# Gate branch as one dense first stage in SBUF, queries made ahead, then attention alone

## The chip, the cores and the metric

The kernel runs on one core of one Trainium2 chip, as one program. The metric is the device time of one execution in microseconds (us), from the first to the last instruction of the core. Lower is better.

## The reference

The input is 2048 tokens of width 512. One layernorm feeds two branches, and the output is `x + s * g`.

```python
x  = A_x                                   # (1, 2048, 512), bf16
xn = layernorm(x)
# branch A, attention: 32 heads of 128, 2048 cached keys and values per head
q  = (xn @ wq) split into heads
p  = softmax(q @ k_cache^T * 128**-0.5)
s  = concat_heads(p @ v_cache) @ wo        # (2048, 512)
# branch B, the gate: token mixer and MLP
h  = gelu(layernorm(xn) @ w1)              # 512 -> 512, tanh form of GELU
hs = [h0 shifted by +1 token, h1 by -1, h2 by +2, h3 by -2] @ w2   # four channel groups of 128
x1 = xn + hs
x2 = x1 + gelu(layernorm(x1) @ w3) @ w4    # 512 -> 1792 -> 512
g  = silu(x2)
out = x + s * g
```

## The kernel before

**Attention.** The work is cut into 128 units, `units`: eight groups `g` of four heads, in each group four blocks `qt` of 512 query tokens, in each block the four heads `hh`. A unit has eight slots, and one loop over `n` walks all slots in order; the program keeps that order on every engine. A slot p of unit u (`s_slot`) makes two score matmuls of 512 columns (`ps_s`, weights from `kT`) and one Exp on ScalarE over the pair, 128x1024, from PSUM into `pT` (L187). Two PSUM buffers hold `ps_s`, so the scores of a slot wait for the Exp two slots earlier. Five slots later (`LAG`) `pv_slot` multiplies by `vb` into `ps_o`.

**Softmax sums.** DVE adds the four `pT` tiles of a unit into `acc` (`add_first`, `add_next`, `add_last`: L193, L198 twice, L203, L204). At p = 3 of the next unit `sums` makes four one-column matmuls with `acc` as weights (`ps_sum`), takes the reciprocal, and sends it through DRAM (`dr`) so that it comes back broadcast to all partitions (`rb`). `norm` (L237) multiplies `ps_o` by `rb` into `oT` at p = 2 of the unit after.

**Queries and output.** `q_mm` makes the query of unit u+1 with four matmuls at p = 0 and 1, and DVE copies it at p = 2 (`q_copy`, L173). When the four heads of a block are done, `wo_mm` and `wo_post` multiply one token tile per unit by `wo` at p = 4 to 6 and add it to `s_acc` (L265); in the last group `wo_post` also multiplies by the gate and adds x (L269, L271) and stores the output. `ps_q`, `ps_sum` and `ps_wo` share one PSUM buffer, tag `xa`.

**The gate.** All matmuls of the mixer and the MLP are cut into 136 chunks (`m1_chunk`, `m2_chunk`, `m3_chunk`, `m4_chunk`) of four or five matmuls, which the slot loop places at p = 2 and 3 or 6 and 7 of units 5 to 119, in PSUM buffer `xm`. A GELU chunk is copied from PSUM by ScalarE (`pre`, L369), and `gelu_pair` then computes the tanh form for a pair of chunks over the next slots: Square on ScalarE (L339), a polynomial on DVE (L343), Tanh on ScalarE (L348), a product on DVE (L351). The layernormed tokens, x1 and the gate each pass through DRAM (`xn_d`, `x1_d`, `g_d`) by DMAs that GpSimd issues; w3 is loaded again for each block of 512 tokens, w4 once.

**Start.** Four token tiles are normalized and transposed by matmuls (`first_tokens`, copies to `xnT` on ScalarE, L314), and the first query is made. Keys are loaded by transposing DMAs on SP's queue (L142). The other twelve token tiles are normalized between the slots of units 0 to 11 and transposed by DMA (L302).

Of the kernel before, what the change touches and what calls it, by code (L numbers as in the profile page):

```python
# [17 lines left out]
def kernel(  # L18
# [15 lines left out]
    nc = tc.nc  # L34
# [7 lines left out]
    assert Dh == P and D % P == 0 and Sq % 512 == 0 and Sk % (2 * P) == 0  # L42
    assert F % (2 * P) == 0 and D == 4 * P
# [7 lines left out]
    HG = 4 if H % 4 == 0 else (2 if H % 2 == 0 else 1)  # L51
# [20 lines left out]
    s_acc = const.tile([P, NT, D], FP32, name="s_acc")  # L72
    ones_t = const.tile([P, 1], BF16, name="ones_t")
    nhalf = const.tile([P, 1], FP32, name="nhalf")
    mv2 = const.tile([P, NT, nc.vector.BN_AGGR_DIM], FP32, name="mv2")
    rstd2 = const.tile([P, NT], FP32, name="rstd2")
    nc.vector.memset(ones_t[:], 1.0)
    nc.vector.memset(nhalf[:], -0.5)
    ident = const.tile([P, P], BF16, name="ident")
    diag = const.tile([P, P], FP32, name="diag")  # L80
    pin(nc.gpsimd.iota(diag[:], pattern=[[-1, P]], base=0, channel_multiplier=1,
# [15 lines left out]
    tokp = ent(pool("tok", 4))
    mp = ent(pool("mp"))
    drp = ent(pool("drp", 4, bass.MemoryType.DRAM))
    dsp = ent(pool("dsp", 1, bass.MemoryType.DRAM))  # L100
    psS = ent(pool("psS", 2, PSUM))
    psO = ent(pool("psO", 2, PSUM))
    psX = ent(pool("psX", 1, PSUM))

    xsrc = x2d.rearrange("(t p) d -> t p d", p=P)
    wq_v = A_wq.rearrange("(dc p) j -> p dc j", p=P)
    w3_v = B_w3.rearrange("(dc p) f -> p dc f", p=P)
    xn_d = [dsp.tile([P, D], BF16, name=f"xn_d{t}") for t in range(NT)]
    x1_d = [dsp.tile([P, D], BF16, name=f"x1_d{t}") for t in range(NT)]
    g_d = [dsp.tile([P, D], BF16, name=f"g_d{t}") for t in range(NT)]  # L110

    def mm(out, lhsT, rhs, start, stop):
        pin(nc.tensor.matmul(out=out, lhsT=lhsT, rhs=rhs, start=start, stop=stop))  # L113

    def rsqrt(out, var):
        ve = smp.tile([P, 1], FP32, name="ve")
        pin(nc.gpsimd.tensor_scalar(out=ve[:], in0=var, scalar1=EPS, scalar2=None, op0=ALU.add))
        pin(nc.gpsimd.tensor_tensor(out=out, in0=ve[:], in1=nhalf[:], op=ALU.pow))
# [40 lines left out]
    def load_wo(h):  # L159
        wos[h] = wop.tile([P, D], BF16, name="wo_h")  # L160
        pin(nc.sync.dma_start(out=wos[h][:], in_=A_wo[h * Dh:(h + 1) * Dh, :]))

    def q_mm(u, dcs):
        g, qt, hh = units[u]
        if dcs[0] == 0:
            st[u] = dict(psq=psX.tile([P, 512], FP32, tag="xa", name="ps_q"))
        for dc in dcs:
            mm(st[u]["psq"][:], wqs[g * HG + hh][:, dc, :],
               xnT[:, dc, qt * 512:(qt + 1) * 512], dc == 0, dc == DC - 1)

    def q_copy(u):
        qT = qtp.tile([P, 512], BF16, name="qT")
        pin(nc.vector.tensor_copy(out=qT[:], in_=st[u].pop("psq")[:]))  # L173
        st[u]["qT"] = qT

    def s_slot(u, p):
# [7 lines left out]
        if p % 2 == 0:  # L184
            s.setdefault("pT", []).append(ptp.tile([P, 4, 512], BF16, name="pT"))
# [20 lines left out]
    def pv_slot(u, p):  # L206
        g, qt, hh = units[u]
        s = st[u]
        if p == 0:
            s["o"] = psO.tile([P, 512], FP32, name="ps_o")  # L210
# [16 lines left out]
    def bcast(u):  # L227
        st[u]["rb"] = rp.tile([P, 512], FP32, name="rb")
# [11 lines left out]
    wo_box = {}  # L240

    def wo_mm(g, t, hhs):
        if hhs[0] == 0:
            wo_box[0] = psX.tile([P, D], FP32, tag="xa", name="ps_wo")
# [7 lines left out]
    def fin_load(t):  # L252
        xl = tokp.tile([P, D], BF16, tag="ta", bufs=8, name="xl")
        nc.gpsimd.dma_start(out=xl[:], in_=xsrc[t])
        gl = tokp.tile([P, D], BF16, tag="ta", bufs=8, name="gl")
        nc.gpsimd.dma_start(out=gl[:], in_=g_d[t][:])
        fin[t] = (xl, gl)

    def wo_post(g, t):
        ps = wo_box.pop(0)  # L260
        sa = s_acc[:, t, :]
        if g == 0:
            pin(nc.vector.tensor_copy(out=sa, in_=ps[:]))
            return
        pin(nc.vector.tensor_tensor(out=sa, in0=ps[:], in1=sa, op=ALU.add))  # L265
        if g < NG - 1:
            return
        xl, gl = fin.pop(t)
        pin(nc.vector.scalar_tensor_tensor(  # L269
            out=gl[:], in0=sa, scalar=0.5, in1=gl[:], op0=ALU.mult, op1=ALU.mult))  # L270
        pin(nc.vector.tensor_tensor(out=xl[:], in0=gl[:], in1=xl[:], op=ALU.add))  # L271
# [3 lines left out]
    ln = {}  # L275

    def ln1_load(t, eng):
        xin = tokp.tile([P, D], BF16, tag="ta", bufs=8, name="xin")
        pin(eng.dma_start(out=xin[:], in_=xsrc[t]))
        ln[t] = xin  # L280

    def ln1_stats(t):
        xin = ln[t]
        bn = smp.tile([P, nc.vector.BN_STATS_DIM], FP32, name="bn")
        mv = smp.tile([P, nc.vector.BN_AGGR_DIM], FP32, name="mv")
        rs = smp.tile([P, 1], FP32, name="rs")
# [5 lines left out]
    def ln1_norm(t):
        xin, mv, rs = ln.pop(t)
        xn = tokp.tile([P, D], BF16, tag="tb", bufs=8, name="xn")
        pin(nc.vector.tensor_scalar(
            out=xn[:], in0=xin[:], scalar1=mv[:, 0:1], scalar2=rs[:],
            op0=ALU.subtract, op1=ALU.mult))
        return xn

    def ln1_apply(t):  # L300
        xn = ln1_norm(t)
        pin(nc.sync.dma_start_transpose(out=xnT[:, :, t * P:(t + 1) * P], in_=xn[:]))  # L302
        pin(nc.gpsimd.dma_start(out=xn_d[t][:], in_=xn[:]))

    def first_tokens():
        xns = [ln1_norm(t) for t in range(4)]
        st[0] = dict(psq=psX.tile([P, 512], FP32, tag="xa", name="ps_q"))
        psq = st[0]["psq"]
        for t in range(4):
            tp = psO.tile([P, DC, P], FP32, tag="ps_o", name="ps_o")  # L310
            for dc in range(DC):
                mm(tp[:, dc, :], xns[t][:, dc * P:(dc + 1) * P], ident[:], True, True)
            ts = slice(t * P, (t + 1) * P)
            pin(nc.scalar.activation(out=xnT[:, :, ts], in_=tp[:], func=ACT.Identity))  # L314
            if t >= 1:
                q_part(t - 1, psq)
        q_part(3, psq)
        qT = qtp.tile([P, 512], BF16, name="qT")
        pin(nc.vector.tensor_copy(out=qT[:, 0:3 * P], in_=psq[:, 0:3 * P]))
        pin(nc.vector.tensor_copy(out=qT[:, 3 * P:], in_=psq[:, 3 * P:]))  # L320
        st[0].pop("psq")
        st[0]["qT"] = qT
        for t in range(4):
            pin(nc.gpsimd.dma_start(out=xn_d[t][:], in_=xns[t][:]))

    def q_part(t, psq):
        ts = slice(t * P, (t + 1) * P)
        for dc in range(DC):
            mm(psq[:, ts], wqs[0][:, dc, :], xnT[:, dc, ts], dc == 0, dc == DC - 1)


    mlp = {}

    def gelu_pair(pre, dest, n):
        sq = gtp.tile([P, 2, 512], BF16, name="sq")
        f2 = "p a f -> p (a f)"

        def square():
            pin(nc.scalar.activation(  # L339
                out=sq[:], in_=pre[:], func=ACT.Square, scale=GELU_A ** 0.5))  # L340

        def poly():
            pin(nc.vector.scalar_tensor_tensor(  # L343
                out=sq[:].rearrange(f2), in0=sq[:].rearrange(f2), scalar=1.0,
                in1=pre[:].rearrange(f2), op0=ALU.add, op1=ALU.mult))

        def tanh():
# [338 lines left out]
```

## Time and profile before

| what | value |
|---|---|
| three runs | 1300.81, 1303.24, 1305.64 us; median 1303.24 |
| profiled execution, first to last instruction (span) | 1303.1 us |
| granted TensorE clock, mean over the span | 0.994 |
| TensorE / ScalarE / DVE / GpSimd busy | 1267.1 / 1113.9 / 1024.7 / 146.4 us |
| matmuls | 6236 |
| DMA | 111.76 MB, mean 86 GB/s |

The span is the profiled execution's own time; it lies within the three runs. In the profile's rows PE is TensorE's matmul pipeline, PEld its weight loads, DVE is VectorE, ACT is ScalarE, POOL is GpSimd and SP is SyncE; a q behind an engine's name means its instruction queue, for instance where it issues a DMA. A row of a timeline has the start and the length of a group of like instructions, both in us, and in brackets the idle time before it and what ended it. A row of the groups has the count, the busy time in us, the mean of one in ns and the idle time before. A row of the table of stretches has the stretch, its length, then busy time and count for PE, PEld, DVE, ACT and POOL, then the granted clock, the DMA share and GB/s. All matmuls have one line, since one helper makes them; they are told apart by their tiles.

### The profile page before, as it was taken

Reading aid. Unit: us, or ns where it says so; the run is one execution under the profiler, and the core shown is the slowest. Engines: PE = TensorE matmul, PEld = TensorE weight load, DVE = VectorE, ACT = ScalarE, POOL = GpSimd, SP = SyncE. Lnnn points to the kernel's source line nnn. Section 1 sums busy time; section 2 is a strip of 40 time slices with the busy share of each in tenths; the row PEclk is TensorE's granted clock in tenths of the full one; section 3 lists DMA queues with packets and bytes.
Section 4 is the critical chain, followed back from the end, with each engine's and each line's share of the span. In section 5 each row is a group of like instructions: output and inputs, shape, how many; then the busy total and the mean of one; then the engine's idle time right before and its main releaser. Section 6 shows DMA issues by size and latency. Waiting matters only on the chain.

```text
span 1303.1 us, 17205 instructions
## 1 busy us (share of the span) xinstructions
PE 1267.1 (97%) x6236; PEld 608.7 (47%) x6236; DVE 1024.7 (79%) x1404; ACT 1113.9 (85%) x1189; POOL 146.4 (11%) x259
## 2 busy tenths in 40 slices
PE   7898999999999999999999999999999999999995
PEld 3444444444444444444444444444444444444442
DVE  5787788888788777788887778888777878777886
ACT  6888998887899988899988889998889999888882
POOL 4223002333111100000001000000000000000110
PEclk9999999999999999999999999999999999999997
DMA  7735343356432555224553245424444224422322
GB/s 174 150 85 118 67 85 89 80 132 138 102 73 81 98 106 90 48 66 81 93 98 62 55 94 87 90 49 86 73 84 91 41 58 76 91 61 54 81 71 71
DMA packets 174292, 111.76 MB, mean 86 GB/s; under 512 B 127040, under 2 KB 151104, under 8 KB 174208
## 3 DMA queue, kind: packets, MB, share of 16 engines
q1 hardware_dynamic: 162176, 82.36, 32.7%
q0 software_dynamic: 9632, 27.54, 8.3%
q10 hardware_dynamic: 2400, 0.79, 0.3%
q8 instruction: 48, 0.79, 0.3%
q14 instruction: 36, 0.29, 0.1%
HBM read 81.53 MB, written 8.65 MB: 69 GB/s over the span
## 4 chain that ended last, share of the span: by engine, by line
PE 83%; DVE 6%; ACT 5%; DMA 3%; issue 1%; SPq 0%; POOL 0%; ACTq 0%; DVEq 0%; POOLq 0%
PE ps_s L113 30%; PE ps_o L113 28%; PE ps_m L113 9%; PE ps_wo L113 9%; PE ps_q L113 7%; ACT pT L187 3%; DVE acc L198 2%; DMA rb<-dr 1%; PE ps_sum L113 1%; ACT sq L339 1%; DMA dr<-rc 1%; DMA kT<-in_A_k_cache_dram 1%; DVE s_acc L265 1%; DVE acc L203 1%; ACT pre L369 1%
## 5 line engine op out<-in xcount | busy, mean ns | idle before, releaser
L187 ACT ACTIVATE pT<-ps_s 128x1024 bf16<-128x1024 f32 x1024 | 1014.7, 1029 | 156.4 <-PE ps_s L113 154.0
L113 PE MATMUL ps_s<-qT,kT 128*128 128x512 bf16 x2048 | 610.0, 380 | 3.8 <-DMA kT<-in_A_k_cache_dram 2.2
L113 PE MATMUL ps_o<-pT,vb 128*128 128x512 bf16 x2048 | 608.3, 379 | 1.3 <-DVE oT L237 1.3
L198 DVE TENSOR_TENSOR acc<-acc,pT 128x2048 bf16<-128x2048 bf16 x256 | 312.2, 1220 | 55.5 <-ACT pT L187 49.7
L113 PEld LDWEIGHTS <-kT 128*128 128x128 bf16 x2048 | 227.0, 113 | 226.0 <-issue 17.6
L113 PEld LDWEIGHTS <-vb 128*128 128x128 bf16 x2048 | 200.0, 98 | 227.0 <-issue 1.6
L193 DVE TENSOR_TENSOR acc<-pT 128x2048 bf16<-128x2048 bf16 x128 | 155.9, 1218 | 29.5 <-ACT pT L187 29.5
L113 PE MATMUL ps_wo<-wo_h,oT 128*128 128x512 bf16 x512 | 154.3, 385 | 8.1 <-DVE oT L237 3.9
L113 PE MATMUL ps_q<-xnT,wq_h 128*128 128x512 bf16 (+1 forms) x524 | 154.1, 379 | 4.9 <-DVE acc L204 2.7
L265 DVE TENSOR_TENSOR s_acc<-ps_wo,s_acc 128x512 f32<-128x512 f32 x112 | 77.2, 690 | 93.5 <-PE ps_wo L113 93.4
L237 DVE TENSOR_TENSOR oT<-ps_o,rb 128x512 bf16<-128x512 f32 x128 | 87.1, 681 | 7.6 <-DMA rb<-dr 7.6
L173 DVE CAST qT<-ps_q 128x512 bf16<-128x512 f32 x127 | 87.0, 685 | 7.1 <-PE ps_q L113 7.1
L203 DVE TENSOR_TENSOR acc<-acc 128x1024 bf16<-128x1024 bf16 x128 | 88.6, 692 | 4.4
L113 PEld LDWEIGHTS <-oT 128*128 128x128 bf16 x512 | 50.4, 99 | 73.0 <-issue 11.9
L113 PEld LDWEIGHTS <-wq_h 128*128 128x128 bf16 x524 | 51.7, 100 | 66.8 <-issue 6.6
L113 PE MATMUL ps_m<-xn2T,w_sb 128*128 128x512 bf16 x224 | 66.5, 378 | 0.0
L113 PE MATMUL ps_m<-w_sb,h2T 128*128 128x512 bf16 x224 | 64.0, 379 | 0.0
L488 POOL DMA_DIRECT2D w_sb<-in_B_w_dram x28 | 21.1, 755 | 352.7 <-PE ps_m L113 327.2
L204 DVE TENSOR_TENSOR acc<-acc 128x512 bf16<-128x512 bf16 x128 | 54.4, 425 | 4.4
L113 PEld LDWEIGHTS <-acc 128*128 128x128 bf16 x512 | 37.0, 115 | 36.4 <-DVE acc L204 6.2
L223 DVE RECIPROCAL rc<-ps_sum 128x4 f32<-128x4 f32 x128 | 22.9, 179 | 37.7 <-PE ps_sum L113 36.7
L520 POOL DMA_DIRECT2D g_d<-xr x16 | 8.7, 546 | 350.5 <-DVE xr L518 350.5
(54 smaller groups left out, 569.6 us busy)
## 6 DMA issues: line engine op xcount, KB each, us to landing
rb<-dr SPq DMA_DIRECT2D x128, 256.0 KB, 4.4
vb<-in_A_v_cache_dram SPq DMA_DIRECT2D x64, 256.0 KB, 4.7
w_sb<-in_B_w_dram POOLq DMA_DIRECT2D x28, 256.0 KB, 4.1
wo_h<-in_A_wo_dram SPq DMA_DIRECT2D x32, 128.0 KB, 4.1
wq_h<-in_A_wq_dram SPq DMA_DIRECT2D x28, 128.0 KB, 4.6
kT<-in_A_k_cache_dram SPq DMA_TRANSPOSE x128, 4.7
xn_d<-xn POOLq DMA_DIRECT2D x16, 128.0 KB, 4.3
dr<-rc SPq DMA_DIRECT2D x128, 2.0 KB, 1.4
```

The source lines that it names most:

```text
L113: pin(nc.tensor.matmul(out=out, lhsT=lhsT, rhs=rhs, start=start, stop=stop))
L173: pin(nc.vector.tensor_copy(out=qT[:], in_=st[u].pop("psq")[:]))
L187: pin(nc.scalar.activation(out=s["pT"][-1][:, jj:jj + 2, :], in_=sps[:], func=ACT.Exp, scale=SCALE))
L193: pin(nc.vector.tensor_tensor(out=s["acc"][:], in0=s["pT"][0][:], in1=s["pT"][1][:], op=ALU.add))
L198: pin(nc.vector.tensor_tensor(out=a[:], in0=a[:], in1=st[u]["pT"][i][:], op=ALU.add))
L203: pin(nc.vector.tensor_tensor(out=a[:, 0:2, :], in0=a[:, 0:2, :], in1=a[:, 2:4, :], op=ALU.add))
L204: pin(nc.vector.tensor_tensor(out=a[:, 0, :], in0=a[:, 0, :], in1=a[:, 1, :], op=ALU.add))
L223: pin(nc.vector.reciprocal(out=rc[:], in_=ps[:]))
L237: pin(nc.vector.tensor_tensor(out=oTs[(g, qt)][:, hh, :], in0=s["o"][:], in1=s["rb"][:], op=ALU.mult))
L265: pin(nc.vector.tensor_tensor(out=sa, in0=ps[:], in1=sa, op=ALU.add))
L339: pin(nc.scalar.activation(out=sq[:], in_=pre[:], func=ACT.Square, scale=GELU_A ** 0.5))
L488: pin(nc.gpsimd.dma_start(out=w[:], in_=w3_v[:, :, fc * P:(fc + 2) * P]))
```

## The change

The gate branch is taken out of the slot loop. A first stage, written out by hand, runs all of m1, m2 and m3 and the m4 of token tiles 0 to 7 before the first score matmul; the m4 of tiles 8 to 15 (`held`) runs in units 0 to 3, three or four matmuls per slot. The queries of units 0 to 15 are made in the first stage and copied by ScalarE; later units make theirs as before. GELU is one ScalarE activation per 128x1024, straight from PSUM (`Gelu_apprx_tanh`), and DVE has no part in it. Normalized tokens, x1 and the gate live in one SBUF tile, `xall`, and no longer pass through DRAM; w3 is loaded once. Twelve matmuls on a tile of zeros run first. The tiles that only the first stage needs and those that only attention needs share SBUF, opened one after the other (`pL` then `pB`, `pR` then `pS`). `ps_wo` moves from PSUM buffer `xa` to `xm`. In the changed instruction order ScalarE loads its function tables three times: before the first copy, before the first GELU and before the first Exp.

The diff, cut to its core:

```diff
+    def tr_pe(t):
+        tp = psO.tile([P, DC, P], FP32, tag="ps_o", name="ps_o")
+        for dc in range(DC):
+            mm(tp[:, dc, :], xall[:, t, dc * P:(dc + 1) * P], ident[:], True, True)
+        pin(nc.scalar.activation(out=xnT[:, :, t * P:(t + 1) * P], in_=tp[:], func=ACT.Identity))
+
+    def tr_dma(t):
+        pin(nc.sync.dma_start_transpose(out=xnT[:, :, t * P:(t + 1) * P], in_=xall[:, t, :]))
+
+    def m1(c0, w):
+        for jp in range(DC // 2):
+            b = BASE_J[2 * jp]
+            ps = psS.tile([P, 2, 512], FP32, name="ps_s")
+            for j in range(2):
+                jc = 2 * jp + j
+                for dc in range(DC):
+                    mm(ps[:, j, 0:w], w1_sb[:, dc, jc * P:(jc + 1) * P],
+                       xnT[:, dc, c0:c0 + w], dc == 0, dc == DC - 1)
+            pin(nc.scalar.activation(
+                out=hT[:, 2 * jp:2 * jp + 2, b + c0:b + c0 + w], in_=ps[:, :, 0:w],
+                func=ACT.Gelu_apprx_tanh))
...
+    def m3(c, f):
+        ps = psS.tile([P, 2, 512], FP32, name="ps_s")
...
+        h2[c, f] = pR.tile([P, 2, 512], BF16, tag="h2T", bufs=FC, name="h2T")
+        pin(nc.scalar.activation(out=h2[c, f][:], in_=ps[:], func=ACT.Gelu_apprx_tanh))
...
-    def q_copy(u):
+    def q_copy(u, eng=None):
         qT = qtp.tile([P, 512], BF16, name="qT")
-        pin(nc.vector.tensor_copy(out=qT[:], in_=st[u].pop("psq")[:]))
+        if eng is None:
+            pin(nc.vector.tensor_copy(out=qT[:], in_=st[u].pop("psq")[:]))
+        else:
+            pin(nc.scalar.activation(out=qT[:], in_=st[u].pop("psq")[:], func=ACT.Identity))
...
-            wo_box[0] = psX.tile([P, D], FP32, tag="xa", name="ps_wo")
+            wo_box[0] = psX.tile([P, D], FP32, tag="xm", name="ps_wo") if ps is None else ps
...
+    for _ in range(12):
+        mm(wps[:], warm[:, 0:P], warm[:], True, True)
...
+    m1(0, 256)
...
+    m1(256, 256)
+    for t in range(8, 12):
+        load_x(t, nc.gpsimd)
...
+    ln1_block(range(4, 8))
+    for t in range(12, 16):
+        load_x(t, nc.gpsimd)
+    for i in range(FC // 2):
+        pin(nc.sync.dma_start(out=w3_sb[i][:], in_=w3_v[:, :, i * 2 * P:(i + 1) * 2 * P]))
+    def q_ahead(u):
+        q_mm(u, range(DC), ("xa", "xm")[u % 2])
+        q_copy(u, nc.scalar)
+
+    for u in range(HG):
+        q_ahead(u)
+    pend = [(t, m2(t)) for t in range(2)]
+    ln1_block(range(8, 12))
+    m1(512, 512)
+    for t, ps in pend:
+        x1(t, ps)
+    for u in range(HG, 2 * HG):
+        q_ahead(u)
+    pend = [(t, m2(t)) for t in range(2, 4)]
+    ln1_block(range(12, 16))
+    m1(1024, 512)
...
+    for h in range(HG):
+        load_k(h, range(KSPLIT))
+        load_v(h, (0, 1))
+        if h == 0:
+            for f in range(FC // 2):
+                m3(0, f)
...
+            for t in range(8, 12):
+                ln2(t)
+        if h == 1:
+            for f in range(FC // 2):
+                m3(1, f)
...
+    for t in range(0, 4):
+        gate_out(t)
+    for f in range(FC // 2):
+        m3(2, f)
+    for t in range(4, 8):
+        gate_out(t)
+    for f in range(FC // 2):
+        m3(3, f)
...
+    held = deque(range(8, 16))
...
+        m4(t, heldps[t], range(FC * i // 4, FC * (i + 1) // 4))
...
-        if u == 0 and p in (0, 2, 4):
-            q_mm(1 + p // 2, range(DC))
-        if u == 0 and p in (1, 3, 5):
-            q_copy(1 + p // 2)
-        if p in (0, 1) and HG - 1 <= u < NU - 1:
+        if p in (0, 1) and 4 * HG - 1 <= u < NU - 1:
             q_mm(u + 1, (2 * p, 2 * p + 1))
...
-        if p in (2, 3, 6, 7):
-            w = 2 * u + (p >= 4)
...
+        held_mm(n)
         for fn in todo.pop(n, ()):
             fn()
```

`ln1_block` computes the statistics and the normalized tile of four token tiles on DVE and transposes them by DMA on SP's queue (`tr_dma`); `gate_out(t)` is the m4 of one token tile, its addition to `xall`, Tanh on ScalarE and the last product on DVE.

More of the change, by code (lines that the diff above doesn't have):

```diff
@@ L50 @@
     SCALE = float(Dh) ** -0.5
-    HG = 4 if H % 4 == 0 else (2 if H % 2 == 0 else 1)
+    HG = 4
     NG = H // HG
@@ new lines, in m2, with x1, ln2 @@
+    def m2(t):
+        ps = psO.tile([P, D], FP32, tag="ps_o", name="ps_o")
+        for jc in range(DC):
+            c0 = BASE_J[jc] + t * P - SHIFT[jc]
+            mm(ps[:], hT[:, jc, c0:c0 + P], w2_sb[:, jc, :], jc == 0, jc == DC - 1)
+        return ps
+    def x1(t, ps):
+        pin(nc.vector.tensor_tensor(out=xall[:, t, :], in0=ps[:], in1=xall[:, t, :], op=ALU.add))
+    def ln2(t):
+        c, ts = divmod(t, 4)
+        if ts == 0:
+            xn2T[c] = pL.tile([P, DC, 512], BF16, tag="xn2T", bufs=2, name="xn2T")
+        y = tokp.tile([P, D], BF16, tag="ta", bufs=10, name="xn2")
+        norm_to(y[:], xall[:, t, :], mv2, rs2, t)
+        pin(nc.sync.dma_start_transpose(out=xn2T[c][:, :, ts * P:(ts + 1) * P], in_=y[:]))
@@ new lines, in x2, with gate_tanh, gate_silu, q_mm @@
+    def x2(t, ps):
+        pin(nc.vector.tensor_tensor(out=xall[:, t, :], in0=ps[:], in1=xall[:, t, :], op=ALU.add))
+    def gate_tanh(t):
+        th = tokp.tile([P, D], BF16, tag="ta", bufs=10, name="th")
+        pin(nc.scalar.activation(out=th[:], in_=xall[:, t, :], func=ACT.Tanh, scale=0.5))
+        return th
+    def gate_silu(t, th):
+        pin(nc.vector.scalar_tensor_tensor(
+            out=xall[:, t, :], in0=th[:], scalar=1.0, in1=xall[:, t, :], op0=ALU.add, op1=ALU.mult))
+    def q_mm(u, dcs, tag="xa"):
@@ L209, in pv_slot @@
         if p == 0:
-            s["o"] = psO.tile([P, 512], FP32, name="ps_o")
+            s["o"] = psO.tile([P, 512], FP32, tag="ps_o", name="ps_o")
         pT = s["pT"][p // 2]
@@ L292, in ln1_norm @@
[L292 to L347, printed above, removed]
-            pin(nc.scalar.activation(out=sq[:], in_=sq[:], func=ACT.Tanh, scale=GELU_C))
-        def last():
-            pin(nc.vector.scalar_tensor_tensor(
-                out=dest, in0=sq[:], scalar=1.0, in1=pre[:], op0=ALU.add, op1=ALU.mult))
-        at(n + 1, square)
-        at(n + 3, poly)
-        at(n + 5, tanh)
-        at(n + 7, last)
@@ L359, in gelu_chunk @@
-    def gelu_chunk(lhs, rhs, j, key, dest):
-        def run(i, n):
-            if i == 0:
-                mlp["ps"] = psX.tile([P, 512], FP32, tag="xm", name="ps_m")
-            for dc in (2 * i, 2 * i + 1):
-                mm(mlp["ps"][:], lhs(dc), rhs(dc), dc == 0, dc == DC - 1)
-            if i == 1:
-                if j == 0:
-                    mlp["pre"] = gtp.tile([P, 2, 512], BF16, name="pre")
-                pre = mlp["pre"]
-                pin(nc.scalar.activation(out=pre[:, j, :], in_=mlp["ps"][:], func=ACT.Identity))
-                if j == 1:
-                    gelu_pair(pre, dest(), n)
-        return run
@@ new lines @@
+    pin(nc.sync.dma_start(out=w2_sb[:], in_=w2_v))
+    wps = psX.tile([P, 512], FP32, tag="xm", name="ps_warm")
+    for _ in range(12):
+        mm(wps[:], warm[:, 0:P], warm[:], True, True)
+    for jc in range(DC):
+        b = BASE_J[jc]
+        pin(nc.gpsimd.memset(hT[:, jc, 0:b], 0.0))
+        pin(nc.gpsimd.memset(hT[:, jc, b + Sq: Sq + PADW], 0.0))
+    ln1_stats(0)
+    ln1_stats(1)
+    ln1_norm(0)
+    tr_pe(0)
+    ln1_stats(2)
+    ln1_norm(1)
+    tr_pe(1)
+    m1(0, 256)
+    ln1_stats(3)
```

424 lines of the change are left out of this document (161 added, 263 removed).

## The prediction

> **What bounds the kernel now.** I read the page first (busy times, slices), then the table of stretches, which I cut where the kinds of units change, and last the timeline of one unit in which no MLP work is left.
>
> ```profile
> span 1303.1 us, 17205 instructions
> PE 1267.1 (97%) x6236; PEld 608.7 (47%) x6236; DVE 1024.7 (79%) x1404; ACT 1113.9 (85%) x1189; POOL 146.4 (11%) x259
> PE   7898999999999999999999999999999999999995
> ```
>
> TensorE is the bound from the fourth slice on; what it loses lies in the first three slices and the last. But a busy PE says only that some matmul is in its pipe, so I need the pace. Two pairs of matmuls in the undisturbed middle of a unit give it:
>
> ```profile
> start us, us, engine line op out<-in xcount [idle before <-releaser]
> 1220.03 0.60 PE L113 MATMUL ps_s<-qT,kT 128*128 128x512 bf16 x2
> ...
> 1228.23 0.59 PE L113 MATMUL ps_o<-pT,vb 128*128 128x512 bf16 x2
> 1229.00 0.27 PE L113 MATMUL ps_sum<-ones_t,acc 128*128 128x1 bf16 x4 [0.18 <-DVE qT L173]
> 1229.13 0.60 PE L113 MATMUL ps_s<-qT,kT 128*128 128x512 bf16 x2
> ```
>
> Between the first and the second row lie 19 pairs, 38 matmuls of 512 columns, in 8.20 us: 0.2158 each. The four small sums of a unit take 1229.13 - 1229.00 = 0.13. The program has 2048 ps_s, 2048 ps_o, 512 ps_q, 512 ps_wo and 576 MLP matmuls (64, 64, 224, 224) of 512 columns, 5696 in all: 5696 x 0.2158 + 128 x 0.13 = 1229.2 + 16.6 = 1245.8 us that neither kernel can shed. The profiled execution's span is 1303.1, the median of the three runs 1303.24; I treat them as the same. So 57.3 us are lost, and the stretches say where:
>
> ```profile
> core 0: us, PE busy (x) PEld busy (x) DVE busy (x) ACT busy (x) POOL busy (x), PEclk, DMA share, GB/s
> 0.00:13.20 13.20, 3.92 (x33) 3.43 (x34) 5.59 (x17) 3.56 (x5) 8.00 (x21) 1.00 0.93 190
> 13.20:134.38 121.18, 111.53 (x530) 52.00 (x530) 95.09 (x141) 103.08 (x112) 35.72 (x60) 1.00 0.56 122
> 134.38:1206.14 1071.76, 1070.19 (x5293) 516.25 (x5292) 847.83 (x1137) 943.33 (x1008) 91.35 (x157) 1.00 0.41 81
> 1206.14:1269.87 63.73, 62.61 (x309) 29.97 (x308) 54.86 (x79) 55.44 (x58) 8.07 (x15) 1.00 0.29 74
> 1269.87:1303.10 33.23, 18.85 (x75) 7.03 (x73) 21.34 (x33) 8.50 (x9) 3.22 (x6) 0.77 0.27 74
> ```
>
> These are: start, units 0 to 11, units 12 to 119, units 120 to 126 (no MLP left), unit 127 with the tail. A unit has four sums, so the second stretch holds 530 - 44 = 486 full matmuls: 486 x 0.2158 + 11 x 0.13 = 106.3, lost 14.9. Likewise the third: 4861 full, 108 units, 1063.0, lost 8.7. The fourth: 281, 7 units, 61.5, lost 2.2. The last: 67, 14.7, lost 18.5. With the start's 13.2 that is 57.5, the whole loss.
>
> **The change, part by part.** Matmul work stays (16 transposes as before; twelve warming matmuls on zeros and a few halves of 256 columns are extra). So the sum is the floor 1245.8 plus the new losses.
>
> *Start.* The old first unit waits for ScalarE, which issues four wq loads before its table load:
>
> ```profile
> 1.66 5.59 ACTq L157 DMA_DIRECT2D wq_h<-in_A_wq_dram  x4
> 7.27 1.28 ACT L314 ACT_TABLE_LOAD   x1 [7.27 <-DMA kT<-in_A_k_cache_dram]
> 8.57 1.08 ACT L314 ACTIVATE xnT<-ps_o 128x512 bf16<-128x512 f32 x2
> 14.00 1.91 PE L113 MATMUL ps_q<-xnT,wq_h 128*128 128x512 bf16 x4
> 15.71 1.91 PE L113 MATMUL ps_s<-qT,kT 128*128 128x512 bf16 x4
> ```
>
> In the changed order the K transposes are no longer ahead, and the last wq issues wait for x tiles instead, but the same loads and the same table load stand before the first copy. Two token tiles must be in xnT (8.57 + 1.08 = 9.65) before the first half of m1; with the earlier release I take 9, between 8.5 and 12 if w1 lands late. The last two rows show something else: from 14.00 to 15.71 four matmuls took 1.71 us, 0.43 each, twice the later pace. The twelve new matmuls would take 12 x 0.43 = 5.1 us at that pace and fit before the transposes, so useful work should begin at full pace. The Trainium skill, "TensorE: Matmul & The Clock Gate", section "What's actually happening", says that PE starts at half clock and is let go after some 3.4 us of sustained work, and gated again after an idle window; the 0.43 here agrees with half clock (the profile's granted clock shows 1.00 there and does not). If the gate closes again before m1, an estimate by that rule adds up to 2 us.
>
> *Bubble between the two halves of m1.* ScalarE loads the GELU table (a second 1.28, from the row above) and then copies tiles 2 and 3: PE has nothing from the third and fourth transposes to the last copy. Two table-free copies 1.08 and some latency: 1.4 us (0.5 to 2).
>
> *First stage.* 528 matmuls of floor work. GELU is one activation of 128x1024 from PSUM per eight matmuls (8 x 0.2158 = 1.73 us), and the nearest rows for it are these:
>
> ```profile
> L187 ACT ACTIVATE pT<-ps_s 128x1024 bf16<-128x1024 f32 x1024 | 1014.7, 1029 | 156.4 <-PE ps_s L113 154.0
> L348 ACT ACTIVATE sq<-sq 128x1024 bf16<-128x1024 bf16 x36 | 38.8, 1078 | 0.0
> L369 ACT ACTIVATE pre<-ps_m 128x512 bf16<-128x512 f32 x72 | 42.8, 595 | 0.8 <-PE ps_m L113 0.8
> w_sb<-in_B_w_dram POOLq DMA_DIRECT2D x28, 256.0 KB, 4.1
> xnT<-xn SPq DMA_TRANSPOSE x12, 4.5
> ```
>
> Exp takes 1.03, Tanh 1.08; GELU at that price is hidden under 1.73 with two PSUM buffers. A query copy on ScalarE costs 0.6 against 0.86 of its four matmuls, with two buffers: hidden. On DVE the square-and-polynomial work goes away. What can show is loading: transposes of token tiles 8 to 11 are queued on SP behind seven w3 loads. PE reaches m1 of these tiles after 80 matmuls, at 9 + 1.4 + 17.3 = 27.7 us. Tiles 4 to 7 are issued by about 16 (estimate from x landing and 1.3 us of DVE a tile), w3 needs some 0.5 us of issue each, the four transposes 1.25 each and 4.5 to land: 16 + 3.5 + 5 + 4.5 = 29. I take 3 us for this and smaller waits (0 to 8). The transposes of ln2's tiles 8 to 11 wait on SP until m3 of block 0 has read its buffer (about 65 us), and K and V of heads 1 to 3 stand behind them: head 1 is wanted only a unit after 127, so some 60 us of m3 and m4 cover this; without that cover each head's K piece costs its landing, 4 to 5 us.
>
> *Seam.* Before the first Exp the last GELU (1.03) must end and a third table load (1.28) run, while PE has only 11 matmuls (2.37 us) before it needs that Exp: (1.03 + 1.28 + 1.03) - 2.37, rounded up for latency, 1.3 (0 to 2.6). The Trainium skill, "ScalarE: Activation LUTs", section "What ACT_TABLE_LOAD costs", gives 1283 ns plus a drain of about 1380 ns for every switch; the trace has the 1.28 and only one load, so no drain between two functions. By the page this term would be 2.7 and the sum 1.4 higher.
>
> *Units 0 to 3* carry the last eight tiles' m4 (7.5 matmuls a slot, 1.62 us): PE-bound, no loss. *Units 4 to 14* have neither queries nor MLP: 32 or 36 matmuls, near ScalarE's pace. The old kernel has one like it, unit 4:
>
> ```profile
> 51.08:59.10 8.02, 8.02 (x41) 3.89 (x40) 6.21 (x9) 7.52 (x9) 1.92 (x4) 1.00 0.87 195
> ```
>
> 36 full matmuls make 7.90, so 0.12 is lost; with wo in the slots instead of q it may be twice that. Unit 4 itself has 32 matmuls, 7.03, against 8 Exps: their pace back to back is 2.86/3 = 0.95 (row below), 7.6. In all 10 x 0.15 + 0.5 = 2 (1 to 4).
>
> *Units 16 to 116: the crux.* 101 units of 40 matmuls, 8.76 us each if nothing waits. The old kernel covers any late DVE with MLP matmuls (units of 44 to 49); only units 120 to 126 have 40, and these lose 2.2/7, by the row 1229.00 exactly 0.34: that row starts 0.77 after 1228.23, where 0.43 was due. Who is late?
>
> ```profile
> 1222.82 0.69 DVE L265 TENSOR_TENSOR s_acc<-ps_wo,s_acc 128x512 f32<-128x512 f32 x1 [1.10 <-PE ps_wo L113]
> 1223.25 2.86 ACT L187 ACTIVATE pT<-ps_s 128x1024 bf16<-128x1024 f32 x3 [0.27 <-PE ps_s L113]
> 1223.55 0.69 DVE L269 SCALAR_TENSOR_TENSOR gl<-s_acc,gl 128x512 bf16<-128x512 f32 x1
> 1224.27 0.43 DVE L271 TENSOR_TENSOR xl<-gl,xl 128x512 bf16<-128x512 bf16 x1
> 1224.62 2.55 DVE L198 TENSOR_TENSOR acc<-acc,pT 128x2048 bf16<-128x2048 bf16 x2
> 1227.20 0.69 DVE L203 TENSOR_TENSOR acc<-acc 128x1024 bf16<-128x1024 bf16 x1
> 1227.92 0.43 DVE L204 TENSOR_TENSOR acc<-acc 128x512 bf16<-128x512 bf16 x1
> 1228.27 0.68 DVE L173 CAST qT<-ps_q 128x512 bf16<-128x512 f32 x1
> ```
>
> From 1222.82 to 1228.95 DVE never rests, and the sums wait for its last step: the query's copy L173, because q and sums share one PSUM buffer. But L269 and L271, 1.07 us, belong to the output and run in the last group alone. Without them the first add starts at 1223.55 and ends at about 1224.8; the second must wait for Exp 7, the second of the three from 1223.25, ending near 1225.2. It then starts 0.65 earlier than now (1225.9), and the sums are free at 1228.35, 0.31 before PE wants them at 1228.66. So I charge nothing, with 0.31 to spare; up to 0.1 a unit (10 us) if some waits recur. That the output units lose 0.34 stays: units 117 to 126, 10 x 0.34 = 3.4.
>
> *Tail* 18.5 as before: the same chain, only without gl's loads.
>
> Sum: 9 + 1.4 + 3 + 1.3 + 2 + 0 + 3.4 + 18.5 = 38.6 over 1245.8: 1284.4, so **1285**. Against 1303: the start gives 4, units 0 to 11 give 15, the MLP's disturbances 9; bubble, loading, seam and ScalarE-paced units take 8, three more output units 1. Low ends (8.5, 0.5, 0, 0, 1, 0, 3.4, 18.5) make 1278; the high ones (12, 2, 8, 2.6, 4, 10, 3.4, 18.5) 1306, not all at once: 1297.
>
> **Rivals.** *A, slower:* MLP matmuls were the cover of the DVE chain, and every bare unit waits 0.34 for its sums as units 120 to 126 do: 1285 + 101 x 0.34 = 1319. It decides if the chain from Exp 7 to L173 grows by more than 0.31 us. For it: the only bare units in the trace do wait. Against: L269 and L271 explain it. *B, no change:* SP's queue takes the w3 loads one at a time, 7 x 4.1 = 28.7 us instead of 3.5; then the transposes land at 54 less some overlap, near 50, not 27.7, and 22 us in place of 3 give 1304. Against: by the instruction order each load waits only for the one eight before it. *C, slower:* Exp paces bare units at its 1029 ns rather than 0.95; then the two pairs of short slots (4 matmuls, 0.863) in each unit lag by 0.17 a slot, some 0.5 a unit after the buffers' slack, 1285 + 55 = 1340. Against: three in 2.86. That the change is not what it says can be left out: the changed instruction order shows GELU from PSUM and three table loads.
>
> **How the numbers follow.** Forecast 0.75, A 0.11, B 0.10, C 0.04. The forecast's cases lie between 1278 and 1297; reaching to 1301 takes part of B and leaves out about 2 in 10. About 0.5% (6.5 us) is what a measurement can tell: faster is below 1296.7, the forecast's 0.75; same is B's 0.10; slower is A and C, 0.15.
>
> **What would show it.** Right: Exp begins near 127 us; the spacing of units 20 to 110 is 8.76 us and the sums wait for nothing; units 117 to 126 stay at 9.10; three table loads. Wrong: sums waiting on L173's successor in every unit (A), PE idle for over 10 us before 50 us with a transpose as releaser (B), S matmuls waiting for Exp in every unit (C).

## The result and the profile after

The changed kernel takes 1289.72 us (four runs, 1289.44 to 1290.44) against 1303.62 for the kernel before (four runs, 1300.81 to 1305.64): ratio 0.989, 95% interval 0.9874 to 0.9906. That is faster by 1.1%, 13.9 us. The profiled execution took 1289.44 us, with a span of 1287.6; some 1.8 us lie around the span. The page of the changed kernel:

```profile
span 1287.6 us, 16764 instructions
...
PE 1257.4 (98%) x6128; PEld 609.6 (47%) x6252; DVE 942.5 (73%) x1316; ACT 1054.8 (82%) x1101; POOL 47.5 (4%) x115
...
PE   7999999999999999999999999999999999999995
```

TensorE's slices read 9 from the second to the last but one, and DVE lost 82 us of work, ScalarE 59, GpSimd 99. Some matmul records are missing here (6128 of 6252), so matmuls are counted by their weight loads, PEld, below. The table of stretches of the changed kernel, cut where the kinds of units change: first stage, units 0 to 3, 4 to 14, 15 to 116, 117 to 126, unit 127 with the tail.

```profile
core 0: us, PE busy (x) PEld busy (x) DVE busy (x) ACT busy (x) POOL busy (x), PEclk, DMA share, GB/s
0.00:129.14 129.14, 121.88 (x561) 56.13 (x573) 58.73 (x132) 55.32 (x67) 39.98 (x101) 0.99 0.59 125
129.14:181.45 52.31, 50.75 (x239) 23.85 (x242) 26.90 (x36) 38.42 (x41) 3.76 (x7) 1.00 0.16 31
181.45:269.57 88.12, 87.24 (x428) 42.44 (x436) 68.18 (x89) 82.56 (x89) 0.54 (x1) 1.00 0.32 64
269.57:1163.72 894.15, 889.42 (x4399) 437.12 (x4487) 690.43 (x919) 791.09 (x816) 0.00 (x0) 1.00 0.37 69
1163.72:1254.71 90.99, 88.95 (x434) 43.00 (x442) 76.87 (x110) 78.83 (x82) 3.22 (x6) 1.00 0.21 51
1254.71:1287.60 32.89, 19.16 (x74) 7.10 (x73) 21.41 (x33) 8.56 (x9) 0.00 (x0) 0.71 0.21 52
```

The fourth row is the crux of the prediction: 102 units of 8.77 us each, with the floor at 8.76. (The row ends 0.35 us before the first matmul of unit 117; the ten units of the fifth row take 90.7 us from start to start.) Loss by the prediction's accounting, counted unit by unit from the trace's weight loads:

| stretch | before, us lost | after, forecast | after, measured |
|---|---|---|---|
| up to the first score matmul | 12.3 (13.2 less the first query's matmuls) | 13.4 (9 + 1.4 + 3) | 15.2 |
| seam, unit 0 | in units 0 to 11, 14.9 | 1.3 | 1.8 |
| units 1 to 3 | same | 0 | 0.5 |
| units 4 to 14 | same | 2 | 2.1 |
| units 15 to 116 | 12 to 119: 8.9 | 0 | 0.8 |
| units 117 to 126 | 120 to 126: 2.4 | 3.4 | 3.1 |
| unit 127, tail | 18.7 | 18.5 | 18.35 |
| sum over 1245.8 | 57.2 | 38.6 | 41.8 |

A bare unit of the changed kernel in the timeline, to be laid beside unit 120 to 126 of before:

```profile
start us, us, engine line op out<-in xcount [idle before <-releaser]
...
601.48 0.69 DVE L365 TENSOR_TENSOR sacc<-ps_wo,sacc 128x512 f32<-128x512 f32 x1 [0.76 <-PE ps_wo L106]
...
601.91 2.86 ACT L283 ACTIVATE pT<-ps_s 128x1024 bf16<-128x1024 f32 x3 [0.27 <-PE ps_s L106]
...
602.09 1.22 DVE L294 TENSOR_TENSOR acc<-acc,pT 128x2048 bf16<-128x2048 bf16 x1
...
603.88 1.23 DVE L294 TENSOR_TENSOR acc<-acc,pT 128x2048 bf16<-128x2048 bf16 x1 [0.58 <-ACT pT L283]
...
605.14 0.69 DVE L299 TENSOR_TENSOR acc<-acc 128x1024 bf16<-128x1024 bf16 x1
...
605.86 0.42 DVE L300 TENSOR_TENSOR acc<-acc 128x512 bf16<-128x512 bf16 x1
...
606.21 0.68 DVE L267 CAST qT<-ps_q 128x512 bf16<-128x512 f32 x1
...
606.89 0.59 PE L106 MATMUL ps_o<-pT,vb 128*128 128x512 bf16 x2
...
607.32 0.27 PE L106 MATMUL ps_sum<-ones_t,acc 128*128 128x1 bf16 x4
```

The second add now waits 0.58 for Exp 7, the query's copy ends at 606.89, and the sums start at 607.32, 0.43 after the last pair, as they should: no wait. What TensorE does wait for (waits of the changed kernel: total us, times, longest):

```profile
PE ps_s L106 <- DMA xnT<-xall: 2.9, 1, 2.9
...
PE ps_s L106 <- ACT xnT L191: 1.9, 2, 1.2
...
PE ps_sum L106 <- DVE qT L267: 1.6, 9, 0.2
...
PE ps_s L106 <- ACT pT L283: 1.2, 2, 0.9
```

The nine waits for L267 are those of units 118 to 126, each 9.10 us long; unit 117 took 8.77. Only some 0.18 of the 0.34 that such a unit loses is counted as a wait.

### The profile page after: what moved, and what is told of

It reads as the page before. It is cut to its first block, busy times and chain, and to the rows that moved or that the text cites. A ratio compares the mean times of both kernels' runs of the same rounds, so it can differ in the third digit from the quotient of the medians.

```text
span 1287.6 us, 16764 instructions
## 1 busy us (share of the span) xinstructions
PE 1257.4 (98%) x6128; PEld 609.6 (47%) x6252; DVE 942.5 (73%) x1316; ACT 1054.8 (82%) x1101; POOL 47.5 (4%) x115
## 4 chain that ended last, share of the span: by engine, by line
PE 89%; DVE 6%; DMA 2%; ACT 1%; issue 1%; POOL 0%; another core or an unknown queue 0%; SPq 0%; DVEq 0%; ACTq 0%
PE ps_s L106 36%; PE ps_o L106 35%; PE ps_wo L106 8%; PE ps_q L106 7%; DVE acc L294 2%; PE ps_m L106 2%; PE ps_sum L106 1%; ACT pT L283 1%; DVE sacc L365 1%; DVE xall L369 1%; DVE acc L299 1%; DMA kT<-in_A_k_cache_dram 1%; DVE qT L267 0%; DVE xl L371 0%; DMA xnT<-xall 0%
## 5 line engine op out<-in xcount | busy, mean ns | idle before, releaser
L283 ACT ACTIVATE pT<-ps_s 128x1024 bf16<-128x1024 f32 x1024 | 993.1, 1026 | 135.3 <-PE ps_s L106 130.4
L106 PE MATMUL ps_s<-qT,kT 128*128 128x512 bf16 x1986 | 596.8, 380 | 3.9 <-ACT pT L283 1.2
L106 PEld LDWEIGHTS <-kT 128*128 128x128 bf16 x2048 | 222.0, 113 | 203.0 <-issue 6.1
L365 DVE TENSOR_TENSOR sacc<-ps_wo,sacc 128x512 f32<-128x512 f32 x112 | 77.4, 691 | 89.5 <-PE ps_wo L106 88.7
L106 PE MATMUL ps_q<-xnT,wq_h 128*128 128x512 bf16 x481 | 141.6, 379 | 0.2
L267 DVE CAST qT<-ps_q 128x512 bf16<-128x512 f32 x112 | 76.3, 682 | 0.0
L355 POOL DMA_DIRECT2D xl<-in_A_x_dram x16 | 8.7, 543 | 1137.4 <-DMA out_dram<-xl 1014.3
L106 PE MATMUL ps_s<-xn2T,w_sb 128*128 128x512 bf16 x220 | 48.6, 379 | 0.2
L106 PEld LDWEIGHTS <-w_sb 128*128 128x128 bf16 x304 | 30.0, 99 | 39.1 <-issue 7.7
L234 ACT ACTIVATE h2T<-ps_s 128x1024 bf16<-128x1024 f32 x28 | 28.7, 1024 | 24.0 <-PE ps_s L106 23.3
```

The lines of the kernel that those rows point to most:

```text
L234: pin(nc.scalar.activation(out=h2[c, f][:], in_=ps[:], func=ACT.Gelu_apprx_tanh))
L283: pin(nc.scalar.activation(out=s["pT"][-1][:, jj:jj + 2, :], in_=sps[:], func=ACT.Exp, scale=SCALE))
```

## The experiments

Runs 1 to 4, 7 and 8 are edits of the changed kernel, 5 and 6 of the kernel before, which took 1302.47 us beside the first four and 1303.73 beside the last four.

**1. The output's two DVE steps moved behind the softmax adds.** Theory: the ten bare units that still lose 0.34 lose it to the output's product and sum, L369 and L371, and not to the missing MLP cover (rival A).

```diff
-    def wo_post(g, t):
+    def wo_post(g, t, n=None):
...
+        def output():
+            pin(nc.vector.scalar_tensor_tensor(
+                out=gl, in0=sa, scalar=0.5, in1=gl, op0=ALU.mult, op1=ALU.mult))
+            pin(nc.vector.tensor_tensor(out=xl[:], in0=gl, in1=xl[:], op=ALU.add))
+            pin(nc.sync.dma_start(out=out2d[t * P:(t + 1) * P, :], in_=xl[:]))
+        if n is not None and n + 7 < NU * SPU:
+            at(n + 7, output)
+        else:
+            output()
```

> Edit of the changed kernel: in the last group the gate product and the addition of x (0.69 + 0.43 us of DVE) are put seven slots later, behind add_first, where DVE now waits for the output matmuls. Theory (the bare units' DVE chain has some 0.3 us to spare, and only these two operations make it late): units 117 to 126 go from 9.11 to 8.77 us each, the sums wait no more, span 3 us shorter than the changed kernel's (about 1284.5, ratio to before 0.986 to 0.987). Rival (the wait of 0.34 comes from the output's DMA or from bare units as such): 9.11 stays and the time is the changed kernel's.

Measured: 1286.35 us (1286.19 to 1286.85), ratio to before 0.9876 (0.9862 to 0.989); span 1284.5, 3.1 under the changed kernel. Its table of stretches for units 117 to 126:

```profile
1164.47:1252.17 87.70, 87.70 (x441) 42.97 (x440) 75.97 (x109) 77.58 (x81) 3.22 (x6) 1.00 0.22 52
```

Ten units in 87.70, 8.77 each, where the changed kernel needs 90.7 from the start of unit 117 to that of unit 127. The same DVE work is done; only its place ahead of the adds cost.

**2. More DVE work in every bare unit.** One extra addition of 128x512 behind `sacc` in groups 1 to 3, two in groups 4 to 6. Theory: there is some slack, then a cliff.

```diff
+        for _ in range((0, 1, 1, 1, 2, 2, 2, 0)[g]):
+            scr = pS.tile([P, D], FP32, tag="scr", bufs=1, name="scr")
+            pin(nc.vector.tensor_tensor(out=scr[:], in0=sa, in1=sa, op=ALU.add))
```

> Edit of the changed kernel: behind every addition to sacc, DVE does one more 128x512 float32 addition of about 0.7 us into a scratch tile in groups 1 to 3, and two in groups 4 to 6. Theory: 1.07 us of extra DVE work costs 0.34 in the output units, so 0.73 is free: groups 1 to 3 stay at 8.77 to 8.85 us a unit, groups 4 to 6 go to about 9.45 (1.44 - 0.73 = 0.7 more). In all about 35 to 40 us. Rival (waits of bare units do not come from the amount of DVE work before the sums): both stay at 8.77. Second rival (no slack at all): 9.5 and 10.2.

Measured in a single run: 1319.02 us, span 1317.2. A unit with one extra addition still takes 8.77 us, one with two 9.37. The group of the additions and the wait that appears:

```profile
L368 DVE TENSOR_TENSOR scr<-sacc 128x512 f32<-128x512 f32 x144 | 99.7, 692 | 4.9
```

```profile
PE ps_sum L106 <- DVE qT L267: 22.9, 57, 0.4
```

With two additions the first softmax add starts 2.06 us after the sum into `sacc` does (1004.00 and 1006.06 in this run's timeline) instead of 0.61 (601.48 and 602.09 above). That is 1.45 us later, and a unit grew by 0.60: so some 0.84 us of delay at this place is free. The output units of the kernel before agree: there the first add starts 1.80 us behind (1222.82 and 1224.62), 1.19 later than in a bare unit of the changed kernel, and 0.34 is lost. Rival A's mechanism is real, then, but it begins more than one addition away from where the changed kernel stands.

**3. One warming matmul instead of twelve.**

```diff
-    for _ in range(12):
+    for _ in range(1):
         mm(wps[:], warm[:, 0:P], warm[:], True, True)
```

> Edit of the changed kernel: one warming matmul in place of twelve. Theory (the first matmuls after idle time run at half pace, 0.43 in place of 0.216 us per 512 columns): the 32 halves of m1 take 0.21 each in place of 0.11, first scores 2 to 4 us later than 129.1, time up by 2 to 4 us less what the wait for token tiles 4 to 7 swallows. Rival (that wait of 3 us swallows all): first scores at 129.1 and the same time.

Measured: 1290.08 us (1289.01 to 1290.68), ratio 0.9904 (0.989 to 0.9918), not to be told from the changed kernel. TensorE's timeline:

```profile
8.55 3.57 PE L106 MATMUL ps_s<-xnT,w_sb 128*128 128x256 bf16 x16 [0.69 <-ACT xnT L191]
...
21.84 3.62 PE L106 MATMUL ps_s<-xnT,w_sb 128*128 128x512 bf16 x16 [0.97 <-DMA xnT<-xall]
...
32.61 3.61 PE L106 MATMUL ps_s<-xnT,w_sb 128*128 128x512 bf16 x16 [1.94 <-DMA xnT<-xall]
```

The first half of m1 does run at half pace, 3.57 us where the changed kernel takes 1.91 (row below). But the m1 of tiles 4 to 7 starts at 21.84 as against 21.75: the late matmuls only shorten a wait for loading, to 0.97 us. The first scores start at 129.66 instead of 129.14. The half pace of the theory came, and the time is the rival's.

**4. Only four queries made ahead.** The other twelve units make theirs in their slots, so the first stage has 48 matmuls, 10.4 us, less.

```diff
-    for u in range(HG, 2 * HG):
-        q_ahead(u)
...
-        if p in (0, 1) and 4 * HG - 1 <= u < NU - 1:
+        if p in (0, 1) and HG - 1 <= u < NU - 1:
             q_mm(u + 1, (2 * p, 2 * p + 1))
```

> Edit of the changed kernel: only the queries of units 0 to 3 are made in the first stage, those of units 4 to 15 in the slot before their unit, as later ones. Theory (units 4 to 14 run at ScalarE's pace and lose 2.1 us for want of matmuls): they go from 8.04 to 8.77 us with four more matmuls each and no loss, the first stage gets 12 x 0.863 = 10.4 us shorter less new waits for the transposes of tiles 8 to 15, since 3.5 us of matmuls ahead of each are gone. Net between 2 us faster and 3 us slower than the changed kernel; first scores at 119 to 123 us. Rival (the queries made ahead are themselves a gain): slower by over 5 us.

Measured: 1295.27 us (1292.44 to 1295.67), ratio 0.9939 (0.9924 to 0.9954); span 1293.5, 5.9 over the changed kernel. The theory missed, and its rival, slower by over 5 us, came true. Units 5 to 15 take about 8.77 and lose almost nothing, as the theory said, which gains 1.9 with unit 4; but the first scores begin at 126.98, only 2.2 earlier instead of 10.4. TensorE's timeline says why:

```profile
31.33 6.24 PE L106 MATMUL ps_s<-xnT,w_sb 128*128 128x512 bf16 x16 [4.58 <-DMA xnT<-xall]
...
51.80 2.83 PE L106 MATMUL ps_o<-w_sb,hT 128*128 128x512 bf16 x12 [2.77 <-DVE xall L217]
```

4.58 idle before the m1 of tiles 8 to 11, 2.6 more for its pace (6.24 where 3.6 is usual), 2.77 before an m2: 10 us that the changed kernel does not lose, against some 2 saved at tiles 4 to 7, where this run waited 2.60 and kept its pace. The first stage loses 8.2 more; the 0.4 that are left of the difference lie in the other units and the tail. The queries are the cover of its loading.

**5. The kernel before, with GELU straight from PSUM left among the Exps.** The same GELU instruction without the separate stage (128x512, as that kernel's chunks are).

```diff
-                    mlp["pre"] = gtp.tile([P, 2, 512], BF16, name="pre")
...
-                pin(nc.scalar.activation(out=pre[:, j, :], in_=mlp["ps"][:], func=ACT.Identity))
-                if j == 1:
-                    gelu_pair(pre, dest(), n)
+                    mlp["pre"] = dest()
+                pin(nc.scalar.activation(
+                    out=mlp["pre"][:, j, :], in_=mlp["ps"][:], func=ACT.Gelu_apprx_tanh))
```

> Edit of the kernel before: each GELU chunk is one ScalarE activation straight from PSUM (128x512), in its place between the Exps; the copy, Square, polynomial, Tanh and product are gone, and the 0.5 in x1 and x2 with them. Theory (GELU from PSUM pays only apart from the Exps, because each change of function loads a table): 72 activations need 144 more table loads of 1.28 us, and as the scores can run only two slots ahead of the Exps, PE waits some 2.5 us for each: 1303 + 72 x 2.5 = about 1480 us, ScalarE busy about 1250. With a drain of 1.38 us on every load, as the Trainium skill states (ScalarE: Activation LUTs, What ACT_TABLE_LOAD costs), about 1680. Rival (the gain of direct GELU does not need the separate stage): 1295 or less.

Measured in a single run: 1436.87 us, span 1434.9. Groups and the wait that carries it:

```profile
L368 ACT ACT_TABLE_LOAD x72 | 92.4, 1283 | 1.3
...
L187 ACT ACT_TABLE_LOAD x72 | 92.4, 1283 | 1.3
...
L368 ACT ACTIVATE h2T<-ps_m 128x512 bf16<-128x512 f32 x56 | 33.5, 597 | 0.6
```

```profile
PE ps_s L113 <- ACT pT L187: 131.8, 72, 2.0
```

Each of the 72 GELUs costs two table loads, and TensorE 1.83 us, less than the 2.5 of the theory. So GELU straight from PSUM, put one chunk at a time among the Exps, costs 133 us. (Several GELUs together between the Exps, and the stage with the long GELU, were not tried.)

**6. The kernel before without the Square and the polynomial of GELU.** Tanh acts on the copied pre-activation, so GELU here is not the reference's; the separate stage is absent.

```diff
-            pin(nc.scalar.activation(out=sq[:], in_=sq[:], func=ACT.Tanh, scale=GELU_C))
+            pin(nc.scalar.activation(out=sq[:], in_=pre[:], func=ACT.Tanh, scale=GELU_C))
...
-        at(n + 1, square)
-        at(n + 3, poly)
```

> Edit of the kernel before: Square on ScalarE and the polynomial on DVE are left out (36 each, 1.07 and 1.22 us), Tanh reads the copied chunk; so the GELU is not the reference's. Theory (the 8.5 us lost in units 16 to 116 come from GELU's extra work on ScalarE, which delays Exps): that loss falls to about 2, time 6 us lower, ratio 0.995; units 0 to 11 stay at 15. Rival (it comes from the MLP's DMAs or its PSUM buffer): the same time.

Measured: 1298.58 us (1297.05 to 1300.86), ratio 0.9962 (0.9948 to 0.9976). Units 12 to 119 lose 2.7 instead of 8.9; units 0 to 11 lose 15.4, as before (14.9). So most of what the changed kernel gains in the middle comes from shortening GELU; whether it is the Square or the polynomial was not separated. For units 0 to 11 the equal loss shows less than it seems to: in this execution two stretches at half pace fall into them (granted clock 0.50 from 47.70 to 51.10 and from 126.20 to 129.60 us), and none at these places in the kernel before. What left those units is the layernorm and the loading of the other twelve tiles. In the trace of the kernel before TensorE waits there 6.0 us for DVE (softmax adds 4.1, `norm` 1.3, the query's copy 0.6) and 3.3 for loads to land (keys 2.2, transposed tokens 1.1), and its first matmuls lose some 2 at half pace; which change removed how much was not tried.

**7. Tiles 4 to 7 transposed by matmuls between the first queries**, in place of the DMA transposes that TensorE waits 3 us for.

```diff
-    ln1_block(range(4, 8))
+    ln1_block(range(4, 8), lambda t: None)
...
     for u in range(HG):
         q_ahead(u)
+        if u >= 1:
+            tr_pe(3 + u)
+    tr_pe(7)
```

> Edit of the changed kernel: token tiles 4 to 7 are transposed by matmuls between the first queries, copied by ScalarE, instead of by DMA on SP's queue, so that w3 and the transposes of tiles 8 to 15 are issued earlier. Theory (PE waits 3.1 us at 18.4 for these transposes, and the idle time puts the next eight matmuls at half pace, 1.7 us): both vanish for 0.9 us of transposes, first scores near 125.3, span about 1283.7, ratio near 0.986. Rival (the wait moves to the next tiles, 8 to 11): first scores at 128 to 130 and the time of the changed kernel.

Measured: 1287.34 us (1287.16 to 1288.77), ratio 0.988 (0.9861 to 0.99); span 1285.4. The m1 of these tiles in TensorE's timeline:

```profile
20.58 3.62 PE L106 MATMUL ps_s<-xnT,w_sb 128*128 128x512 bf16 x15
```

It starts 1.17 earlier, waits for nothing and keeps full pace; the first scores start at 126.29, 2.9 before the changed kernel's. That is less than the theory gave (125.3). The tail is 0.6 longer, which no part of the edit explains; among runs 1 to 4 it varies by 0.5.

**8. Edits 1 and 7 together.**

> Edit of the changed kernel: the two last ones that act on its own losses together, the output's DVE work seven slots later and tiles 4 to 7 transposed by matmuls. Theory: the gains add, 3.1 + 3.9 = 7 us under the changed kernel, ratio to before 0.983 to 0.984. Rival (they share a bottleneck): that of the better one alone, 0.986.

Measured: 1283.86 us (1283.5 to 1284.0), ratio 0.9849 (0.9833 to 0.9866); span 1282.2. Both stretches of its table show their own gain:

```profile
0.00:126.20 126.20, 121.06 (x577) 56.82 (x589) 58.54 (x132) 57.23 (x71) 39.97 (x101) 1.00 0.61 123
...
1161.11:1248.81 87.70, 87.23 (x432) 42.96 (x440) 75.94 (x109) 77.58 (x81) 3.22 (x6) 1.00 0.23 52
```

-2.9 and -3.0, given back by 0.56 in the tail: 5.4 less span than the changed kernel. The gains add, but with the sizes that runs 1 and 7 measured (3.4 and 2.4 us), not to the 7 of the theory. It is the best version of the study, 1.5% under the kernel before.

## Why the prediction was right, and where its terms were off

The forecast was 1285 with 1278 to 1301 around it; 1289.72 came. Of the 4.7 us between, 3.2 are in the span (41.8 lost instead of 38.6), and 1.8 lie around it, less 0.6 by which the sum's 1284.4 was rounded up: the prediction set the execution's time equal to its span, and that term was missing.

**The crux** held: bare units lose nothing once L269 and L271 of the old kernel are out of the chain. The changed kernel shows it in 102 units, run 1 shows it by moving the two steps, run 2 by adding one and two steps like them. The spare is larger than the 0.31 of the prediction: 0.84 by run 2, near the 0.31 and the second add's wait for Exp (0.58 above) together, since what is put ahead of that add uses up its wait first. Rival A is refuted as the state of this kernel, not as a mechanism.

**The first stage** was the term mis-sized: 15.2 for 13.4, so that the first scores start at 129.14 where its terms gave 127.3. Start and bubble came as forecast: useful work from 8.15 (9), and 1.4 between the halves of m1. The loading wait has the forecast's size (3.1 for 3, counting the matmul's own issue), but by luck: the 3 were meant for tiles 8 to 11 and smaller waits, and TensorE waits at tiles 4 to 7. The prediction never set these tiles against its own figures: issued by 16 and 4.5 us to land makes 20.5, while 40 matmuls after 9 + 1.4 bring TensorE to them at 19.0. The changed kernel's timeline from 8 to 27 us:

```profile
8.12 1.28 ACT L205 ACT_TABLE_LOAD   x1
...
8.15 1.91 PE L106 MATMUL ps_s<-xnT,w_sb 128*128 128x256 bf16 x16 [0.69 <-ACT xnT L191]
...
8.87 2.40 POOL L153 DMA_DIRECT2D xin<-in_A_x_dram  x4
...
11.72 1.91 PE L106 MATMUL ps_s<-xnT,w_sb 128*128 128x256 bf16 x16 [1.22 <-ACT xnT L191]
...
12.21 0.41 DVE L177 TENSOR_SCALAR xall<-xin,mv,rs 128x512 bf16<-128x512 bf16 x1 [1.24 <-POOL rs L168]
...
12.65 5.23 SPq L194 DMA_TRANSPOSE xnT<-xall  x4
...
17.93 5.12 SPq L423 DMA_DIRECT2D w_sb<-in_B_w_dram  x7
...
21.75 5.30 PE L106 MATMUL ps_s<-xnT,w_sb 128*128 128x512 bf16 x16 [2.94 <-DMA xnT<-xall]
```

As I read it from the trace (it was not tried by itself), GpSimd issues four x loads from 8.87 to 11.27, the rsqrt of tile 4 stands behind them, and DVE idles 1.24 before it can normalize that tile. The first transpose goes out at 12.65, the issue of the fourth ends at about 17.9, it lands at 21.51, and m1 begins at 21.75. So GpSimd's part is at most 1.24 of the 3.1; the rest is some 1.3 us of SP's queue for each transpose and 4.9 for the fourth to land. The prediction listed SP's queue and not GpSimd's. After the wait, sixteen matmuls take 5.30 instead of 3.62 (run 3's row): from 22.83 on they are 0.427 apart, and back at 0.216 after 26.24. These 1.7 us were in no term. The granted clock shows them, in the table of stretches of the changed kernel:

```profile
22.80:26.30 3.50, 3.50 (x10) 1.28 (x9) 3.23 (x8) 1.03 (x1) 1.38 (x4) 0.51 1.21 294
```

The prediction weighed the gate, the halving of TensorE's clock, at the start of the kernel only. The Trainium skill, "TensorE: Matmul & The Clock Gate", section "What's actually happening", names an idle window of about 3.4 us after which the clock is halved. The runs agree in kind, but not on a length: the changed kernel lost its pace after 3.32 us between the starts of two matmuls, and run 1 kept it after 3.40. Of the 15.2 there remain 0.8 for small waits and transposes.

Yet the 1.7 us are hardly a loss of their own. Runs 1 and 2 have the same first stage and kept full pace after the same wait, and their first scores start at 129.46 and 129.07, not 1.7 earlier. TensorE's timeline of run 1:

```profile
22.08 3.61 PE L106 MATMUL ps_s<-xnT,w_sb 128*128 128x512 bf16 x16 [3.02 <-DMA xnT<-xall]
...
32.42 3.61 PE L106 MATMUL ps_s<-xnT,w_sb 128*128 128x512 bf16 x16 [1.52 <-DMA xnT<-xall]
```

What the full pace saved was waited for at tiles 8 to 11. In the changed kernel the last of their transposes lands at 31.79, and this m1 starts at 32.10 without a wait. So the wait that the prediction named does exist, right behind the other; in the changed kernel the half pace covers it. In both, and in runs 2 and 3 too, the first scores come 97.0 us after this m1.

Run 7 takes the wait and the half pace at tiles 4 to 7 away together, issues the later transposes earlier, and gets 2.9 of 4.8. Most of the other 1.9 is in its timeline: the four tiles' transposes are 16 small matmuls of some 0.06, 0.9 in all, and there is a 0.70 wait for their last copy.

**Rival B** looked for the right wait, TensorE for a transpose, but it is 2.94 us and not over 10: the seven w3 issues took 5.12, more than the forecast's 3.5 and far from 28.7. **Rival C**: three Exps still take 2.86.

**The seam** cost 1.8 for 1.3: the last GELU starts 0.26 us after the first scores (129.14) and not with them. In the changed kernel's timeline:

```profile
129.40 1.02 ACT L234 ACTIVATE h2T<-ps_s 128x1024 bf16<-128x1024 f32 x1 [0.70 <-PE ps_s L106]
...
130.45 1.28 ACT L283 ACT_TABLE_LOAD   x1
...
131.74 3.81 ACT L283 ACTIVATE pT<-ps_s 128x1024 bf16<-128x1024 f32 x4
...
132.82 0.59 PE L106 MATMUL ps_s<-qT,kT 128*128 128x512 bf16 x2 [0.88 <-ACT pT L283]
```

GELU, load and Exp follow one another with 0.03 and 0.01 us between. The drain of some 1380 ns that the Trainium skill gives for each switch ("ScalarE: Activation LUTs", "What ACT_TABLE_LOAD costs") is not in this trace, nor in run 5, where 144 loads stand after 2.6 us of idle time in all and the next activation follows 0.01 us behind each; the load itself is 1283 ns as the page has it. The price of GELU was taken from Exp and came out so:

```profile
L283 ACT ACTIVATE pT<-ps_s 128x1024 bf16<-128x1024 f32 x1024 | 993.1, 1026 | 135.3 <-PE ps_s L106 130.4
...
L234 ACT ACTIVATE h2T<-ps_s 128x1024 bf16<-128x1024 f32 x28 | 28.7, 1024 | 24.0 <-PE ps_s L106 23.3
```

**Output units**: nine lose 0.34, not ten, and **units 4 to 14** and **the tail** came within 0.2. Run 4 shows the size of the ScalarE-paced units from the other side: with the queries back in their slots they lose 0.2 instead of 2.1.

## What to carry to other kernels

Cover is a property of a place, not of an engine's busy share: the MLP matmuls covered little in units whose DVE chain had 0.84 us to spare, and the queries covered a great deal in a stage that waits for loading; ask of each piece of work moved what else was late beside it. Take pace from the spacing of counted matmuls in a unit, since TensorE's slices read 9 nearly everywhere in both kernels. Before you count a wait as a gain to be had, look at what would be late next: full pace after the first wait only lengthened the second. Put steps on which nothing hangs behind the chain (run 1); to put small steps on which a chain hangs ahead of DMA issues on their queue is what the trace suggests, and no run tried it.

## What the runs showed of the hardware

Whether TensorE falls to half pace after a wait does not follow from the length of the wait. Between the starts of two matmuls there were 2.32 (run 3), 2.98 and 3.14 (run 4), 3.06 (run 2), 3.09 (kernel before) and 3.40 us (run 1) without any loss of pace afterwards; after 2.41 and 2.76 (run 6), 3.32 (changed kernel) and 4.96 (run 4) matmuls ran 0.427 apart. Run 1 and the changed kernel have the same first stage, so one execution may keep the pace where another loses it; what decides stays open. The slow pace lasted 3.4 us in the changed kernel and twice in run 6, and some 5.3 in run 4, half of it lost each time. It did not begin with the first matmul in the changed kernel: five ran at 0.216 before it. The granted clock reads 0.51 there, but at the very start, where the warming matmuls are 0.427 apart from 1.58 to 5.42 us, it reads 1.00; at a start only the spacing shows the gate.
